# Retention and two feed-forward layers: loads in rows of 2 KB, a new order of the beginning, zeros in wide products

## The chip, the cores and the metric

One core of one Trainium2 chip. The metric is the device time of one execution in microseconds (us), median of several runs. TensorE is called PE, VectorE DVE, ScalarE ACT, GpSimd POOL, SyncE SP; SP issues nearly all DMAs.

## The reference

Retention (attention without softmax, with a decaying causal mask) for 4 batches, 8 heads, 576 positions, head size 64, then two feed-forward layers on the 2304 tokens with 512 features and 2048 hidden values. All inputs are float32.

```python
scores = q @ k.T / sqrt(64)
ret = scores * where(rel >= 0, gamma[h] ** rel, 0)
x = (ret @ v) as tokens x 512
h = x @ w_in;  g = maximum(0.01 * h, h);   x = g @ w_out      # layer 1
h = x @ w_in2; g = h * cos(h);             out = g @ w_out2   # layer 2
```

## The kernel before, in words

Tokens go through retention in 18 chunks of 128 (ch0 to ch17), the first layer in 5 blocks of up to 512 tokens and 16 slices of the hidden width (f = 0 to 15), the second layer by a scheme with fewer products, whose operands are sums of quarters. Each float32 operand of a feed-forward product is split into a high and a low part of a rounded type, and one product is three (low times high, high times low, high times high). The weights arrive as 64-bit words that ACT and DVE turn into these parts.

The order of the instructions of each engine up to the end of the first block is written out by hand as a table of step names, FIRST; each name issues a few instructions, and the engines run them in that order, held by semaphores alone. What follows is set by a planner, which the change leaves as it is. The steps, for chunk or slice n:

- ch: load of a chunk (lines 238 to 241): q, k in two layouts and v, 1 MB; chunk 0 in two halves. sq, sv: scaling of q and v (lines 247 and 254 or 259).
- s: scores on PE (line 295), 16 products of 64x64. m: times the mask, on DVE (line 316). v: mask times values, PE (line 333). g: growth of the state, PE (line 357). st: the state's sum, DVE (lines 379 and 381). r: what the queries read of the state, PE (line 396) in two parts, with an empty GpSimd instruction behind each part that orders them (line 282). tk: result from PSUM to SBUF, ACT (line 435).
- raw, abs, lo, cs, or, add, hi, low: load of a weight slice (lines 463 and 468; slices 0 and 15 in halves a and b), and its change into parts: abs, lo and hi on ACT (lines 479, 483, 512), cs, or, add and low on DVE (lines 487 and 489, 496, 503, 515).
- xh, xl: high and low part of the layer's input (lines 527 on ACT, 531 on DVE). H: first product of slice n (line 543). lk, gh, gl: the nonlinearity and its parts (lines 568 and 573 on ACT, 578 on DVE). O: second product (line 557). V: a whole retention chunk between products.
- ~n: n products of zeros that only keep PE busy (line 453).

A matmul on float32 leaves two matmul and two weight-load records in the trace, one on the rounded type one of each.

Of the kernel before, what the change touches and what calls it, by code (L numbers as in the profile page):

```python
# [11 lines left out]
I64 = mybir.dt.int64  # L12
# [23 lines left out]
C = P // 2  # L36
# [14 lines left out]


FIRST = """
ch0 sq0 sv0 s0 m0 raw0a abs0a cs0a ~3 v0 or0a ch1 sq1 g0 ch2 ~5 s1 st0.0 st0.1 r0.0 r0 lo0a add0a m1 sv1 v1
sq2 s2 g1 hi0a low0a m2 sv2 v2 g2 ch3 sq3 s3 st1.0 st1.1 r1.0 r1 m3 sv3 v3 g3 raw0b tk0 abs0b cs0b st2.0 st2.1
lo0b or0b add0b r2.0 r2 st3.0 st3.1 tk1 raw1 abs1 cs1 lo1 or1 add1 ~3 r3.0 tk2 r3 tk3 xh0 xl0 ~14 H0.0 xh1 xl1
H0.1 xh2 xl2 H0.2 hi0b low0b xh3 xl3 hi1 low1 raw2 raw3 raw4 ch4 abs2 cs2 H0.3 H1.0 H1.1 H1.2 H1.3 lk0 gh0
abs3 gl0 or2 lo2 add2 lk1 gh1 gl1 sq4 O0 O1 hi2 low2 H2.0 H2.1 H2.2 H2.3 cs3 or3 lo3 add3 abs4 cs4 sv4 V3 raw5
raw6 raw8 hi3 low3 lk2 H3.0 H3.1 H3.2 H3.3 gh2 gl2 O2 or4 lo4 add4 abs5 cs5 hi4 low4 raw7 lk3 gh3 gl3 or5 lo5
add5 abs6 cs6 H4.0 H4.1 H4.2 H4.3 O3 raw9 ch5 lo7 hi5 low5 or6 lk4 gh4 gl4 lo6 add6 H5.0 H5.1 H5.2 H5.3 O4  # L60
st4.0 sq5 hi6 low6 abs7 cs7 lk5 gh5 gl5 or7 add7 m4 H6.0 H6.1 lo8 abs8 st4.1 H6.2 H6.3 lk6 gh6 O5 gl6 O6 hi7
low7 cs8 or8 add8 raw10 abs9 cs9 raw11 raw15a raw12 H7.0 H7.1 H7.2 H7.3 sv5 V4 hi8 lo9 low8 or9 add9 lk7 gh7
gl7 abs10 cs10 hi9 low9 H8.0 H8.1 H8.2 H8.3 lk8 gh8 or10 gl8 st5.0 O7 lo11 abs11 cs11 lo10 add10 ch6 H9.0 H9.1
H9.2 H9.3 lk9 m5 gh9 O8 gl9 O9 hi10 low10 st5.1 raw13 or11 sv6 add11 sq6 tk4 abs12 cs12 H10.0 H10.1 H10.2
H10.3 hi11 V5 ch7 lk10 lo12 low11 m6 st6.0 gh10 gl10 lo13 lo15a H11.0 H11.1 H11.2 H11.3 lk11 gh11 abs13 or12
add12 hi12 gl11 O10 O11 st6.1 cs13 low12 raw15b raw14 or13 add13 H12.0 H12.1 H12.2 H12.3 tk5 sq7 sv7 V6 hi13
low13 abs14 cs14 lk12 lo14 gh12 gl12 or14 add14 H13.0 H13.1 H13.2 H13.3 abs15a lk13 lo15b gh13 gl13 O12 O13
hi14 low14 abs15b st7.0 cs15a cs15b st7.1 m7 or15a tk6 ch8 H14.0 H14.1 H14.2 H14.3 add15a hi15a low15a sq8 sv8
V7 st8.0 or15b lk14 gh14 gl14 st8.1 add15b H15.0 H15.1 H15.2 H15.3 lk15 gh15 gl15 hi15b low15b tk7 O14 O15 m8
ch9 sq9 sv9  # L70
"""


# [99 lines left out]
def retention_ffn_ffn(  # L173
# [7 lines left out]
    nc = tc.nc  # L181
# [31 lines left out]
    tabs_sb = const.tile([P, sum(sizes)], F32, name="tabs_sb")  # L213
# [6 lines left out]
    still = const.tile([P, P], F32, name="still")  # L220
    psum = psp.tile([P, 8, 512], F32, name="psum")
# [3 lines left out]
    n_first = len(chunks[0])  # L225
    n_busy = n_first + len(chunks[1])
# [22 lines left out]
    def scale_v(i):  # L249
        c = i % CYCLE * H  # L250
        if i in (1, 2) or n_first <= i < n_busy:
            for h in range(H):
                v = ch_t[i][:, 3, h * D : (h + 1) * D]
                nc.scalar.activation(v, v, AF.Copy, scale=vtab_sb[:, c + h : c + h + 1])
            return
        v3 = ch_t[i][:, 3].rearrange("p (h d) -> p h d", h=H)
        t3 = vtab_sb[:, c : c + H].unsqueeze(2).to_broadcast([P, H, D])
        eng = nc.gpsimd if 0 < i < n_busy + 2 else nc.vector
        eng.tensor_tensor(out=v3, in0=v3, in1=t3, op=ALU.mult)

    xr, p_t, summed = {}, {}, {}
# [15 lines left out]
    def in_turn(ins, behind):  # L277
        tc.add_manual_dep(ins.ins, behind.ins.name, IN_TURN, reason="same banks")
# [7 lines left out]
    last_of = {}  # L286
# [350 lines left out]
    for j in range(NB - 1):  # L639
        s1 = NF * j + FIRST_CHUNK  # L640
# [4 lines left out]
    def rest():  # L645
# [3 lines left out]
        bank = [psum[:, x, :W] for x in range(8)]  # L649
# [387 lines left out]
        def convert(f, c, tb, due, old):  # L1037

            rb, o = raw_ring.next(), c % 2 * 2 * P
            t_of = lambda: tb.ap[:, o : o + 2 * P]  # L1040
            sides = lambda: rb.ap.bitcast(U32).rearrange("p (x t) -> p x t", t=2)
            lo, hi = lambda: sides()[:, :, 0], lambda: sides()[:, :, 1]

            def load():
                nc.sync.dma_start(rb.ap.bitcast(I64), w[1, f, :, c * 2 * P : (c + 1) * 2 * P])

            def both(op):
                u = t_of().bitcast(U32)
# [24 lines left out]
            return t
# [461 lines left out]
```

## Time and profile before

| | |
|---|---|
| median of 3 runs | 841.66 us (838.97 to 842.35) |
| the profiled execution's own time | 840.51 us |
| its span, first to last instruction | 838.4 us |
| mean granted PE clock | 0.992 |
| PE busy | 812.5 us |
| DVE, ACT busy | 647.3 us, 543.7 us |
| POOL busy | 6.2 us |

The span is what the views below measure; 2.1 us of the execution lie around it. A busy share is an average over stages with different limits: the change touches the first tenth of the span most.

### The profile page before, as it was taken

Reading aid. Unit: us, or ns where it says so; the run is one execution under the profiler, and the core shown is the slowest. Engines: PE = TensorE matmul, PEld = TensorE weight load, DVE = VectorE, ACT = ScalarE, POOL = GpSimd, SP = SyncE. Lnnn points to the kernel's source line nnn. Section 1 sums busy time; section 2 is a strip of 40 time slices with the busy share of each in tenths; the row PEclk is TensorE's granted clock in tenths of the full one; section 3 lists DMA queues with packets and bytes.
Section 4 is the critical chain, followed back from the end, with each engine's and each line's share of the span. In section 5 each row is a group of like instructions: output and inputs, shape, how many; then the busy total and the mean of one; then the engine's idle time right before and its main releaser. Section 6 shows DMA issues by size and latency. Waiting matters only on the chain.

```text
span 838.4 us, 16145 instructions
## 1 busy us (share of the span) xinstructions
PE 812.5 (97%) x6168; PEld 746.0 (89%) x6168; DVE 647.3 (77%) x1147; ACT 543.7 (65%) x1041; POOL 6.2 (1%) x9
## 2 busy tenths in 40 slices
PE   6999999999999999999999998999999999999996
PEld 4877878887888888999999998999999999999996
DVE  4899987887886867786741278799896988877994
ACT  4687866655655456565542498877778876688761
POOL 0000011000000000000000000000000000000000
PEclk9799999999999999999999999999999999999999
DMA  8755325877778767876679499888866677465633
GB/s 319 297 206 208 140 107 189 260 244 215 264 238 254 249 214 258 262 233 217 209 246 416 154 333 328 299 318 312 291 228 254 242 314 289 156 256 197 257 138 114
DMA packets 88636, 203.78 MB, mean 243 GB/s; under 512 B 9072, under 2 KB 54896, under 8 KB 79472
## 3 DMA queue, kind: packets, MB, share of 16 engines
q1 hardware_dynamic: 88416, 202.41, 68.7%
q8 instruction: 48, 0.79, 0.4%
q10 hardware_dynamic: 144, 0.35, 0.1%
q14 instruction: 28, 0.23, 0.1%
HBM read 147.42 MB, written 55.31 MB: 242 GB/s over the span
## 4 chain that ended last, share of the span: by engine, by line
PE 66%; DMA 12%; DVE 11%; ACT 5%; issue 3%; SPq 2%; POOL 0%; DVEq 0%; ACTq 0%; POOLq 0%
PE psum L1362 19%; PE psum L1190 18%; PE psum L543 13%; PE psum L557 13%; DMA more<-in_w 2%; DMA ch<-in_qkv 2%; DMA mraw<-in_w 2%; SPq L933 1%; DMA mt<-y 1%; DMA y<-graw 1%; PE psum L396 1%; DMA ws<-ws 1%; DMA xq<-mt 1%; PE psum L333 1%; PE psum L453 1%
## 5 line engine op out<-in xcount | busy, mean ns | idle before, releaser
L543 PE MATMUL psum<-x_sb,w 128*128 128x512 f32 (+1 forms) x960 | 212.3, 370 | 2.1 <-ACT graw L837 1.4
L557 PE MATMUL psum<-g,w 128*128 128x512 f32 (+1 forms) x960 | 211.9, 370 | 1.2 <-DVE graw L800 0.6
L543 PEld LDWEIGHTS psum<-x_sb,w 128*128 128x128 f32 x960 | 174.5, 188 | 28.2 <-ACT graw L837 2.8
L557 PEld LDWEIGHTS psum<-g,w 128*128 128x128 f32 x960 | 174.1, 188 | 26.5 <-DVE graw L800 1.4
L1190 PE MATMUL psum<-x,ws 128*128 128x384 f32 x576 | 112.2, 335 | 3.6 <-DMA ws<-ws 2.1
L1190 PEld LDWEIGHTS psum<-x,ws 128*128 128x128 f32 x576 | 100.7, 188 | 5.0 <-DMA ws<-ws 2.5
L1362 PE MATMUL psum<-g,wp 128*128 128x384 f32 x432 | 84.4, 339 | 4.0 <-ACT g L1265 2.1
L1190 PE MATMUL psum<-x,wa 128*128 128x384 f32 x432 | 85.5, 335 | 0.5 <-ACT r L1245 0.5
L844 DVE TENSOR_TENSOR g<-graw,g 128x512 fp32r<-128x512 f32 (+1 forms) x64 | 39.8, 622 | 56.5 <-ACT g L841 55.8
L1362 PE MATMUL psum<-g,wq 128*128 128x384 f32 x432 | 82.3, 334 | 0.1
L1362 PEld LDWEIGHTS psum<-g,wp 128*128 128x128 f32 x432 | 75.9, 189 | 6.2 <-ACT g L1265 2.4
L1190 PEld LDWEIGHTS psum<-x,wa 128*128 128x128 f32 x432 | 75.7, 188 | 1.1 <-ACT r L1245 0.8
L1362 PEld LDWEIGHTS psum<-g,wq 128*128 128x128 f32 x432 | 75.5, 188 | 0.4 <-DVE acc L1399 0.4
L837 ACT ACTIVATE graw<-psum 128x512 f32<-128x512 f32 (+1 forms) x64 | 34.7, 542 | 48.9 <-PE psum L543 45.0
L841 ACT CAST g<-graw 128x512 fp32r<-128x512 f32 (+1 forms) x64 | 36.2, 566 | 43.3 <-PE psum L557 43.1
L1399 DVE TENSOR_TENSOR acc<-psum,acc 128x384 f32<-128x384 f32 x90 | 49.6, 554 | 17.2 <-PE psum L1362 16.9
L1248 DVE SCALAR_TENSOR_TENSOR h<-r,h 128x768 f32<-128x768 f32 x48 | 45.7, 952 | 15.2 <-ACT r L1245 15.1
L1261 DVE TENSOR_TENSOR g<-tq,g 128x768 fp32r<-128x768 f32 x48 | 45.6, 953 | 6.8 <-ACT g L1265 6.2
L1239 DVE SCALAR_TENSOR_TENSOR r<-r,h 128x768 f32<-128x768 int32 x48 | 45.5, 951 | 1.9 <-ACT r L1234 1.6
L1244 ACT ACTIVATE r<-r 128x768 f32<-128x768 f32 x48 | 40.6, 847 | 8.7 <-DVE r L1239 8.6
L1234 ACT CAST r<-h 128x768 int32<-128x768 f32 x48 | 40.1, 835 | 8.2 <-DVE h L1220 7.9
L1265 ACT CAST g<-tq 128x768 fp32r<-128x768 f32 x48 | 40.1, 838 | 5.7 <-DVE tq L1282 4.2
(115 smaller groups left out, 1061.0 us busy)
## 6 DMA issues: line engine op xcount, KB each, us to landing
ws<-ws SPq DMA_DIRECT2D x20, 1024.0 KB, 5.2
wp<-wp SPq DMA_DIRECT2D x20, 1024.0 KB, 6.7
ch<-in_qkv SPq DMA_DIRECT2D x17, 1024.0 KB, 6.4
x<-xq SPq DMA_DIRECT2D x21, 768.0 KB, 9.7
wa<-wa SPq DMA_DIRECT2D x20, 768.0 KB, 6.4
wq<-wq SPq DMA_DIRECT2D x20, 768.0 KB, 6.6
raw<-in_w SPq DMA_DIRECT2D x14, 1024.0 KB, 8.8
mraw<-in_w SPq DMA_DIRECT2D x32, 256.0 KB, 4.2
```

Of the source, the lines that this page charges most:

```text
L543: nc.tensor.matmul(hp, wt[:, i, cols], x_t[lj, k][:, j, :n], start=(k == 0 and a == 0), stop=(k == KK - 1 and a == 2),)
L557: nc.tensor.matmul(psum[:, BANK_O + m, :n], wt[:, i, cols], gt[:, j, :n], start=(f == 0 and a == 0), stop=(f == NF - 1 and a == 2),)
L844: nc.vector.tensor_tensor(out=g.ap[:, 1, :n], in0=y.ap[:, :n], in1=g.ap[:, 0, :n].bitcast(F32), op=ALU.subtract)
L1190: nc.tensor.matmul(bank[BANKS[m]].rearrange("p (q t) -> p q t", t=Q), a[:, hl, i, j * P : (j + 1) * P], x[:, :, v, j, :], start=m in (1, 5 ...
L1234: "ACT", 885, lambda: nc.scalar.copy(rb.ap.bitcast(I32), pair()),
L1239: nc.vector.scalar_tensor_tensor(out=rb.ap, in0=rb.ap.bitcast(I32), scalar=-1.0, in1=pair(), op0=ALU.mult, op1=ALU.add)
L1244: t = add("ACT", 885, lambda: nc.scalar.activation(rb.ap, rb.ap, AF.Sin, scale=PI), [t], due)
L1248: nc.vector.scalar_tensor_tensor(out=pair(), in0=rb.ap, scalar=0.5, in1=pair(), op0=ALU.subtract, op1=ALU.mult)
L1261: nc.vector.tensor_tensor(out=gb.ap[:, :, 1], in0=src(), in1=gb.ap[:, :, 0].bitcast(F32), op=ALU.subtract)
L1265: h_ = add("ACT", 885 if n == 2 else 515, lambda: nc.scalar.copy(gb.ap[:, :, 0], src()), [*needs, opened["all"]], due, 0, gb.old)
L1362: nc.tensor.matmul(to, wt[:, hl, i, t * P : (t + 1) * P], gt[:, fi, v, :], start=m in (1, 5) and h == 0 and x == 0, stop=h == 1 and x == 2 ...
L1399: x = add("DVE", 560, lambda: nc.vector.tensor_tensor(out=kept(), in0=to, in1=kept(), op=ALU.add), [got], due - SOON / 2)
```

## The change

Five things. The host lays chunks and weights out in blocks, so that a load of 1 MB takes four rows of 2 KB for each partition from four places, where it took one row of 8 KB (halves: two rows of 2 KB, not one of 4 KB). A second-layer load of 256 KB, which took rows of 2 KB out of rows of 8 KB, now takes one contiguous block. The table FIRST has another order. The load of chunk 4 gets an order behind the last growth product issued so far. The scaling of chunk 3's v goes from GpSimd to DVE. And zeros are multiplied up to 512 columns at a time, with the tables as the moving operand (the stationary one is zero).

```diff
-            nc.sync.dma_start(ch[:, :2], qkv[i, :, :2])
-            nc.sync.dma_start(ch[:, 2:], qkv[i, :, 2:])
+            nc.sync.dma_start(ch[:, :2], qkv[i, :2].rearrange("x p d -> p x d"))
+            nc.sync.dma_start(ch[:, 2:], qkv[i, 2:].rearrange("x p d -> p x d"))
         else:
-            nc.sync.dma_start(ch, qkv[i])
+            got = nc.sync.dma_start(ch, qkv[i].rearrange("x p d -> p x d"))
+            if i == n_first:
+                in_turn(got, last_of["grown"])
...
-        eng = nc.gpsimd if 0 < i < n_busy + 2 else nc.vector
+        eng = nc.gpsimd if n_busy <= i < n_busy + 2 else nc.vector
...
-        for _ in range(n):
-            nc.tensor.matmul(psum[:, bank, :P], still, still, start=True, stop=True)
+        while n > 0:
+            c = min(n, 4) * P
+            nc.tensor.matmul(psum[:, bank, :c], still, tabs_sb[:, C : C + c], start=True, stop=True)
+            n -= 4
...
-        return nc.sync.dma_start(raw, w[0, f])
+        return nc.sync.dma_start(raw.rearrange("p (c t) -> p c t", c=4), w[0, f].rearrange("c p t -> p c t"))
...
-        return nc.sync.dma_start(raw, w[l, f, :, s * DM : (s + 1) * DM])
+        return nc.sync.dma_start(
+            raw.rearrange("p (c t) -> p c t", c=2), w[l, f, 2 * s : 2 * s + 2].rearrange("c p t -> p c t")
+        )
...
-                nc.sync.dma_start(rb.ap.bitcast(I64), w[1, f, :, c * 2 * P : (c + 1) * 2 * P])
+                nc.sync.dma_start(rb.ap.bitcast(I64), w[1, f, c])
...
-ch0 sq0 sv0 s0 m0 raw0a abs0a cs0a ~3 v0 or0a ch1 sq1 g0 ch2 ~5 s1 st0.0 st0.1 r0.0 r0 lo0a add0a m1 sv1 v1
+ch0 sq0 s0 sv0 m0 raw0a abs0a cs0a or0a ~3 v0 g0 st0.0 st0.1 ~4 r0.0 ch1 sq1 s1 r0 lo0a add0a ch2 m1 sq2 sv1
...
```

The order of PE from the scores of chunk 2 on, before (L295 scores, L333 values, L357 growth, L396 reads, L453 zeros):

```order
L295 MATMUL psum<-ch 64x64 x16
L357 MATMUL psum<-ch 64x64 x16
L333 MATMUL psum<-p_sb,ch 64x64 x16
L357 MATMUL psum<-ch 64x64 x16
L295 MATMUL psum<-ch 64x64 x16
L396 MATMUL psum<-ch,st 64x64 x16
L333 MATMUL psum<-p_sb,ch 64x64 x16
L357 MATMUL psum<-ch 64x64 x16
L396 MATMUL psum<-ch,st 64x64 x16
L453 MATMUL psum<-still 128x128 x3
L396 MATMUL psum<-ch,st 64x64 x16
L453 MATMUL psum<-still 128x128 x14
```

And in the changed kernel, from the same scores on (there L297, L335, L359, L398 and L456):

```order
L297 MATMUL psum<-ch 64x64 x16
L398 MATMUL psum<-ch,st 64x64 x8
L335 MATMUL psum<-p_sb,ch 64x64 x16
L398 MATMUL psum<-ch,st 64x64 x8
L359 MATMUL psum<-ch 64x64 x16
L297 MATMUL psum<-ch 64x64 x16
L398 MATMUL psum<-ch,st 64x64 x16
L335 MATMUL psum<-p_sb,ch 64x64 x16
L359 MATMUL psum<-ch 64x64 x16
L456 MATMUL psum<-tabs_sb,still 128x512
L456 MATMUL psum<-tabs_sb,still 128x128
L398 MATMUL psum<-ch,st 64x64 x16
```

The scores of chunk 3 are the second row of scores in each list. The reads of chunk 1 and all growth of chunk 2 now stand ahead of them; zeros that stood in three and fourteen products of 128 columns stand in four of 512 and two of 128, the last four of the six behind these rows.

The order of DVE around the mask multiply of chunk 3 (L316), before; L247 is q's scaling, L381 the state's sums, t_426 and t_464 the weights of slice 0's second half and slice 1 on their way:

```order
L316 TENSOR_TENSOR p_sb<-psum,tabs_sb 128x512
L247 TENSOR_TENSOR ch<-ch,tabs_sb 128x512
L381 TENSOR_TENSOR st<-psum,st 128x256 x2
L316 TENSOR_TENSOR p_sb<-psum,tabs_sb 128x512
L487 TENSOR_SCALAR t_426<-t_426 128x512
L489 TENSOR_SCALAR t_426<-t_426 128x512
L381 TENSOR_TENSOR st<-psum,st 128x256 x2
L496 SCALAR_TENSOR_TENSOR t_426<-raw,t_426 128x512
L503 ISA t_426<-raw,t_426 128x1024
L381 TENSOR_TENSOR st<-psum,st 128x256 x2
```

And in the changed kernel (mask L318, scaling L249 and L261, sums L383; the weights are t_394 and t_477):

```order
L318 TENSOR_TENSOR p_sb<-psum,tabs_sb 128x512
L249 TENSOR_TENSOR ch<-ch,tabs_sb 128x512
L261 TENSOR_TENSOR ch<-ch,tabs_sb 128x512
L383 TENSOR_TENSOR st<-psum,st 128x256 x2
L318 TENSOR_TENSOR p_sb<-psum,tabs_sb 128x512
L494 TENSOR_SCALAR t_394<-t_394 128x512
L496 TENSOR_SCALAR t_394<-t_394 128x512
L503 SCALAR_TENSOR_TENSOR t_394<-raw,t_394 128x512
L510 ISA t_394<-raw,t_394 128x1024
L383 TENSOR_TENSOR st<-psum,st 128x256 x2
```

Two pairs of state sums and the scaling of chunk 3's v now stand ahead of the mask multiply of chunk 3; one pair stands behind it, where two stood.

DVE somewhat later, before: L531 is xl, L515 the low part of a weight slice, L578 the low part of the nonlinearity's result, L247 the scaling of chunk 4:

```order
L531 TENSOR_TENSOR x_sb<-xr,x_sb 128x512 x3
L515 TENSOR_TENSOR w_296<-t_426,w_296 128x512
L531 TENSOR_TENSOR x_sb<-xr,x_sb 128x512
L515 TENSOR_TENSOR w_536<-t_464,w_536 128x1024
L487 TENSOR_SCALAR t_547<-t_547 128x1024
L489 TENSOR_SCALAR t_547<-t_547 128x1024
L578 TENSOR_TENSOR g<-graw,g 128x512
L496 SCALAR_TENSOR_TENSOR t_547<-raw,t_547 128x1024
L503 ISA t_547<-raw,t_547 128x2048
L578 TENSOR_TENSOR g<-graw,g 128x512
L247 TENSOR_TENSOR ch<-ch,tabs_sb 128x512
L515 TENSOR_TENSOR w_606<-t_547,w_606 128x1024
```

And in the changed kernel (L538, L522, L585, L249):

```order
L538 TENSOR_TENSOR x_sb<-xr,x_sb 128x512 x2
L249 TENSOR_TENSOR ch<-ch,tabs_sb 128x512
L538 TENSOR_TENSOR x_sb<-xr,x_sb 128x512 x2
L522 TENSOR_TENSOR w_509<-t_477,w_509 128x1024
L494 TENSOR_SCALAR t_516<-t_516 128x1024
L496 TENSOR_SCALAR t_516<-t_516 128x1024
L585 TENSOR_TENSOR g<-graw,g 128x512
L503 SCALAR_TENSOR_TENSOR t_516<-raw,t_516 128x1024
L510 ISA t_516<-raw,t_516 128x2048
L585 TENSOR_TENSOR g<-graw,g 128x512
```

The scaling of chunk 4 has moved from behind two results of the nonlinearity to between the second and the third low part of x.

## Rows read from the trace of the kernel before

**Rows 1.** The page: PE's busy time and instructions, and the instruction queue (packets, MB, share).

```profile
PE 812.5 (97%) x6168; PEld 746.0 (89%) x6168; DVE 647.3 (77%) x1147; ACT 543.7 (65%) x1041; POOL 6.2 (1%) x9
...
q8 instruction: 48, 0.79, 0.4%
```

**Rows 2.** Busy us by engine (PE, weight loads, DVE, ACT, POOL), granted clock, DMA share, GB/s.

```profile
0.00:9.88 9.88, 6.97 (x93) 3.82 (x96) 2.71 (x6) 2.29 (x4) 0.20 (x4) 1.00 0.79 282
0.00:15.30 15.30, 11.12 (x218) 7.33 (x221) 7.79 (x15) 6.31 (x18) 0.20 (x4) 1.00 0.87 330
0.00:18.51 18.51, 13.78 (x348) 9.61 (x348) 9.91 (x19) 8.38 (x26) 0.20 (x4) 1.00 0.89 335
...
22.20:32.40 10.20, 9.28 (x162) 8.26 (x163) 9.27 (x15) 6.82 (x17) 1.04 (x1) 0.50 0.59 212
50.67:86.25 35.58, 35.58 (x255) 28.43 (x256) 34.35 (x40) 28.61 (x40) 0.00 (x0) 1.00 0.42 153
86.25:838.40 752.15, 735.61 (x5253) 684.96 (x5251) 576.90 (x1055) 483.47 (x934) 4.99 (x4) 1.00 0.70 242
```

**Rows 3.** PE in order of time: start, duration, line, operation, records, idle time before.

```profile
17.94 0.57 PE L295 MATMUL psum<-ch 64*64 64x64 f32 x22
...
21.52 0.38 PE L295 MATMUL psum<-ch 64*64 64x64 f32 x9 [3.02 <-issue]
...
29.79 4.64 PE L453 MATMUL psum<-still 128*128 128x128 f32 x28
...
50.67 2.83 PE L543 MATMUL psum<-x_sb,w 128*128 128x512 f32 x11 [0.39 <-DVE w L515]
```

**Rows 4.** DMA view of 12.9:14.0, 15.3:19.2, 19.2:20.4 and 23.1:24.3, in this order.

```profile
q8 instruction: 1, 0.02, 5.4%
...
q1 hardware_dynamic: 264, 1.44, 101.6%
...
q8 instruction: 1, 0.02, 5.0%
...
q8 instruction: 1, 0.02, 4.8%
```

**Rows 5.** DMA view of 30:34 (8 KB rows), 131.1:132 (2 KB rows), 140:141.2 (2 KB rows, with stores).

```profile
DMA packets 230, 1.70 MB, mean 426 GB/s; under 512 B 22, under 2 KB 22, under 8 KB 22
...
DMA packets 93, 0.33 MB, mean 366 GB/s; under 512 B 16, under 2 KB 16, under 8 KB 65
...
q1 hardware_dynamic: 93, 0.33, 89.7%
...
DMA packets 239, 0.44 MB, mean 364 GB/s; under 512 B 26, under 2 KB 26, under 8 KB 239
```

**Rows 6.** DVE in order of time, columns as in PE's.

```profile
9.79 0.43 DVE L487 TENSOR_SCALAR t<-t 128x512 f32<-128x512 f32 x1 [0.71 <-ACT t L479]
...
17.19 0.69 DVE L247 TENSOR_TENSOR ch<-ch,tabs_sb 128x512 f32<-128x512 f32 x1 [0.70 <-DMA ch<-in_qkv]
...
22.00 0.69 DVE L316 TENSOR_TENSOR p_sb<-psum,tabs_sb 128x512 f32<-128x512 f32 x1 [3.26 <-PE psum L295]
...
22.61 1.13 DVE L487 TENSOR_SCALAR t<-t 128x512 f32<-128x512 f32 x1
...
26.84 0.95 DVE L381 TENSOR_TENSOR st<-psum,st 128x256 f32<-128x256 f32 x2 [0.35 <-PE psum L396]
...
38.54 0.69 DVE L578 TENSOR_TENSOR g<-graw,g 128x512 fp32r<-128x512 f32 x1 [1.32 <-ACT g L573]
...
40.62 1.23 DVE L503 CUSTOM_DVE_ANT_0 t<-raw,t 128x2048 uint16<-128x2048 uint16 x1 [0.25 <-ACT raw L483]
...
49.40 1.22 DVE L515 TENSOR_TENSOR w<-t,w 128x1024 fp32r<-128x1024 f32 x1
```

**Rows 7.** GpSimd in order of time.

```profile
22.41 1.04 POOL L259 TENSOR_TENSOR ch<-ch,tabs_sb 128x512 f32<-128x512 f32 x1 [21.97 <-PE psum L396]
```

**Rows 8.** DMA view of 25.5:25.9: a load issued on an idle queue, median us to landing.

```profile
raw<-in_w SPq DMA_DIRECT2D x1, 1024.0 KB, 5.5
```

More of the change, by code (lines that the diff above doesn't have):

```diff
@@ L53 @@
 FIRST = """
-ch0 sq0 sv0 s0 m0 raw0a abs0a cs0a ~3 v0 or0a ch1 sq1 g0 ch2 ~5 s1 st0.0 st0.1 r0.0 r0 lo0a add0a m1 sv1 v1
[L55 to L68, printed above, removed]
@@ L69 @@
-V7 st8.0 or15b lk14 gh14 gl14 st8.1 add15b H15.0 H15.1 H15.2 H15.3 lk15 gh15 gl15 hi15b low15b tk7 O14 O15 m8
-ch9 sq9 sv9
+ch0 sq0 s0 sv0 m0 raw0a abs0a cs0a or0a ~3 v0 g0 st0.0 st0.1 ~4 r0.0 ch1 sq1 s1 r0 lo0a add0a ch2 m1 sq2 sv1
+hi0a low0a v1 g1 s2 st1.0 st1.1 r1.0 sv2 m2 v2 r1 ch3 sq3 sv3 raw0b raw1 tk0 g2 st2.0 st2.1 s3 m3 abs0b tk1
+cs0b or0b lo0b add0b r2.0 r2 v3 g3 st3.0 st3.1 ~5 r3.0 r3 abs1 cs1 or1 lo1 hi0b low0b add1 tk2 tk3 xh0 xl0 xh1
+xl1 ch4 sq4 xh2 xl2 xh3 xl3 hi1 low1 raw2 raw3 abs2 cs2 ~13 H0.0 H0.1 H0.2 H0.3 H1.0 H1.1 H1.2 H1.3 lk0 gh0
@@ new lines @@
+gl0 lo2 abs3 or2 add2 lk1 gh1 O0 gl1 O1 cs3 hi2 low2 H2.0 H2.1 H2.2 H2.3 sv4 V3 raw4 lo3 or3 add3 abs4 cs4 hi3
+low3 raw5 raw7 raw6 raw8 ch5 raw9 raw15a or4 lk2 gh2 gl2 lo4 add4 abs5 cs5 H3.0 H3.1 H3.2 H3.3 O2 hi4 lk3 low4
+H4.0 H4.1 H4.2 H4.3 gh3 gl3 O3 lo5 or5 add5 abs6 cs6 hi5 lk4 gh4 low5 H5.0 H5.1 H5.2 H5.3 gl4 O4 lo7 lo6 abs7
+or6 add6 cs7 hi6 low6 lk5 gh5 gl5 or7 add7 H6.0 H6.1 H6.2 H6.3 O5 abs8 cs8 hi7 lk6 low7 H7.0 H7.1 H7.2 gh6 gl6
+st4.0 or8 lo8 add8 st4.1 raw10 lo10 sq5 raw11 H7.3 lk7 gh7 gl7 m4 O6 O7 hi8 low8 H8.0 H8.1 abs9 abs10 lo9 sv5
@@ new lines @@
+cs9 or9 add9 raw12 cs10 hi9 low9 H8.2 H8.3 V4 ch6 or10 lk8 gh8 st5.0 gl8 st5.1 add10 abs11 cs11 H9.0 H9.1 H9.2
+H9.3 lk9 gh9 gl9 O8 O9 or11 tk4 hi10 low10 H10.0 H10.1 H10.2 H10.3 raw15b raw13 lo11 add11 raw14 sv6 sq6 m5 V5
+ch7 abs12 hi11 lk10 gh10 cs12 low11 gl10 or12 lo12 add12 lo13 abs13 H11.0 H11.1 H11.2 H11.3 lk11 gh11 hi12 sv7
+lo14 cs13 gl11 st6.0 m6 st6.1 sq7 O10 O11 tk5 low12 H12.0 or13 add13 hi13 H12.1 H12.2 H12.3 lk12 gh12 abs14
+low13 abs15a gl12 V6 st7.0 st7.1 cs14 or14 H13.0 H13.1 H13.2 H13.3 add14 lk13 gh13 gl13 O12 O13 cs15a hi14
@@ L71 @@
+low14 or15a abs15b tk6 lo15b cs15b ch8 H14.0 H14.1 H14.2 H14.3 sq8 sv8 lo15a m7 add15a hi15a low15a V7 st8.0
+lk14 gh14 gl14 st8.1 tk7 H15.0 H15.1 H15.2 H15.3 O14 lk15 or15b add15b gh15 gl15 hi15b low15b O15 m8 ch9 sq9
+sv9
 """
@@ L1500 @@
     parts += [tokens(a).reshape(NCH, P, DM) for a in (k, v)]
-    arrays = {"in_qkv": np.ascontiguousarray(np.stack(parts, axis=2))}
+    arrays = {"in_qkv": np.ascontiguousarray(np.stack(parts, axis=1))}
     layers = []
@@ L1508 @@
         w_out = inputs[f"{name}_w_out"].reshape(NF, P, DM)
-        layers.append(np.concatenate([w_in, w_out], axis=2))
+        layers.append(np.concatenate([w_in, w_out], axis=2).reshape(NF, P, 4, 2 * P).transpose(0, 2, 1, 3))
     arrays["in_w"] = np.ascontiguousarray(np.stack(layers)).view(np.int64)
```

## The prediction

> **What bounds the kernel now.** I read the page first, then PE's busy time by stretches, then PE's timeline of the first 50 us, and last the DVE timeline of the same stretch. PE is busy 97% of the span [rows 1]. From 50.67 to 86.25 us it has no idle time at all, and from 86.25 to the end it is busy 735.61 of 752.15 us [rows 2]. So whatever moves PE's first products of the first layer earlier moves the end by nearly the same amount, and what the change does to transfers behind that point costs nothing as long as PE finds its data there.
>
> The beginning is another matter. The first product with weight tile 3 (step H3, line 543) runs at full pace only from 50.67, released by DVE's subtraction of line 515 [rows 3, 6]. In front of that lies the largest stall. At 18.51 PE stops in the middle of the scores of chunk 3 (32 records, of which 22 have run), and it goes on at 21.52, 3.02 us later, with the releaser "issue": no semaphore that the profile shows ended it [rows 3].
>
> Count instructions: PE plus weight-load records are 189 at 9.88, 439 at 15.30 and 696 at 18.51 [rows 2], so they are some 250 apart. On the instruction queue q8 one packet starts behind each of these: one between 12.9 and 14.0, none between 15.3 and 19.2, one between 19.2 and 20.4, one between 23.1 and 24.3 [rows 4]. Over the span q8 has 48 packets for 2 x 6168 records [rows 1], 257 for each. I read this so: at each boundary of about 256 instructions PE asks for the block after the next one, and at 18.51 the block asked for at 15.3 has not come. By its share of the window a packet takes 5.4% x 1.1 us x 16 = 0.95 us [rows 4], so the second one ends near 20.3, and PE runs 1.2 to 1.3 us later. From asking to running on: 9.88 to about 13.95 + 1.3 = 15.25, that is 5.4 us; 15.3 to 21.52, 6.2 us, both behind 8 KB rows; on an idle queue 21.52 to 24.1 + 1.3, 3.9 us.
>
> **The change, part by part.**
>
> *Rows of 2 KB.* In a stretch of 8 KB rows alone the queue moves 426 GB/s [rows 5]. With 2 KB rows I have two bounds: 366 GB/s at 89.7% busy, 408 at full, and 364 in a stretch in which stores run too [rows 5]. So a load is 4 to 17% longer. Chunk 3, released at 17.19 [rows 6] after some 15 us of queue, comes 0.6 to 2.5 us later. That is hidden by the missing block as long as the scores of chunk 3 can't run before about 21; if that cover went, up to 2 us of it would show. I take 1 us, the end nearer to the load-only row: the scores could then start at 18.9. For the second layer's 256 KB loads the rows stay at 2 KB and only lie together: nothing, either way, since PE's waits there are not for them.
>
> *What the rows do to the fetch.* Bounds: 6.2 us as now, 3.9 us as on an idle queue. I take 5.4 us, the better of the two loaded fetches.
>
> *Zeros in wide products.* 25 narrow products of 4 records (two matmuls, two weight loads) become 8: 68 instructions fewer. In the new order 688 instructions stand ahead of the scores of chunk 3 (before: 652), so the block boundary near 700 falls at their start, not in their middle; the one at about 952 falls on the reads of chunk 3. The stall isn't ordered away. The columns are nearly the same (13 x 128 ahead of H0, 14 x 128 before), so as time they cost what they did.
>
> *The order.* The boundary near 448 is again crossed in the scores of chunk 2, at about 15.6 (15.3, with chunk 2 some 0.3 us later). Plus 5.4: the scores of chunk 3 run from 21.0. They need 0.7 us, so the mask multiply (m3, line 316) starts on DVE at 21.75, against 22.00 [rows 6].
>
> From there DVE sets the pace up to H3: in the old trace from 22.00 to 49.40 + 1.22 = 50.62, 28.62 us [rows 6]. In this chain:
> - one pair of state sums (as the one at 26.84, 0.95 us, about 0.9 of it in the chain) now stands ahead of m3, since the reads of chunk 1 precede the scores of chunk 3: -0.9;
> - the clamp at 22.61 takes 1.13 us where the same form takes 0.43 [rows 6], beside GpSimd's multiply at 22.41 [rows 7]; v's scaling goes to DVE, ahead of the scores, where DVE waits anyway: -0.7;
> - the wait of 0.35 at 26.84 for the reads of chunk 2, which are now done long before: -0.35;
> - the wait of 1.32 at 38.54 is for ACT's rounding of H0's result. H0 started only after the fourteen zero products, at 34.4 (29.79 + 4.64), because they ran at half clock: 22.20 to 32.40 is 0.50 granted [rows 2, 3]. With the clock up the zeros end about 8.5 us after m3 (worked out with the first rival) and H0 is done before DVE comes to it: -1.32; the wait of 0.25 at 40.62 goes with the earlier weights: -0.25.
> - Chunk 4's q scaling is in the chain before and after, only earlier: 0.
>
> Sum: -3.5, so 25.1 us, and H3 runs from 21.75 + 25.1 = 46.9 instead of 50.67: 3.8 us. Behind it PE has no idle time to lose or win up to 86 us, and the order of PE's products is the same from about 80 us on. The profiled execution took 840.51 (838.4 and 2.1 around it), 1.15 below the median of 841.66; it becomes 836.7, and the median **837.9**.
>
> **The rivals.**
>
> *The clock falls as before.* PE still idles, by my sum, from 18.9 to 21.0, and a shorter wait for the reads' block follows near 24. [...] Of the fourteen's 4.64 us, 2.6 lay before 32.40 and 2.0 behind [rows 2, 3], so one costs 0.24 at full clock and 0.48 at half. With the clock up PE needs 8.5 us from m3 to the zeros' end: reads, values and growth of chunks 2 and 3 some 4.2, eighteen zero products' worth of columns 4.3. DVE's turn at H0's result was 15.2 us behind m3 (38.54 less 1.32 and 22.00 [rows 6]); less 0.9, 0.7 and 0.35, plus 0.6 for chunk 4's scaling, it is 13.9, and H0 with ACT's two passes takes 4.1, so H0 has 1.3 us to spare. At half clock throughout it is 3.0 us late; with the clock back at 32.40, 1.9. I take 2.5: gain 3.8 - 2.5 = 1.3, median 840.4. For it: this is what followed 3.02 us of idle time. Against: the idle time is a third shorter, and reads and values follow it at once.
>
> *The fetch is no quicker, or the stop has another cause.* With 6.2 us m3 is at 22.55 and H3 at 47.65, gain 3.0: 838.7; together with the fallen clock 841.2. If something else than a missing block stops PE in these scores and does so for 3.0 us again, it is from 18.9 to 21.9, and the time is the same within 0.1. For that: nothing in the trace names the cause. Against: the packet whose end lies 1.2 us ahead of the restart [rows 3, 4]. [...] The stop right there speaks against it, so I give that half of it 0.03.
>
> *The fetch is as quick as on an idle queue.* 3.9 us: block there at 19.5, scores then, m3 at 20.25, H3 at 45.35: gain 5.3, 836.3. [...] Against: of the two fetches behind 8 KB rows one was 0.8 us quicker than the other, so row size isn't all of the wait.
>
> *Slower.* The load of chunk 4 now waits for the growth products of chunk 3 and then stands ahead of the weights; its q scaling stands on DVE between x's second and third low part, in front of everything that H0 to H3 need. Issued at about 24.6, with the 5.5 us that a load on an idle queue takes [rows 8] it is there at 30.1; DVE comes to it about 31.8 (13.9 us behind m3 less 3.8 of work between). From 1.7 us later on, DVE and all behind it wait one for one: the gain of 3.8 is gone when the chunk lands 5.5 us late. For it: loads here have taken far longer behind others. Against: it is at the head of an empty queue. At 10 us late: 837.9 + 8.3 = 846.2.
>
> **How the numbers follow.** My forecast 0.45, clock falls 0.25, fetch no quicker (with or without the clock) 0.12, quick fetch 0.12, slower 0.06. The forecast's own range is 836.5 to 839.5, by a fetch of 5 to 6 us. For 8 in 10 I take 835.3 (the quick fetch, and the sum's waits a little larger) to 841.2 (fallen clock and a fetch no quicker). About 0.5%, 4.2 us, is what a measurement of this kernel can tell from no change; that is below 837.5. The quick fetch and the better two fifths of the forecast are there: 0.33. Slower by that takes the last rival and little else: 0.06. The rest is 0.61.
>
> **What would show it.** Right: PE's "issue" wait at the scores of chunk 3 is near 2 us instead of 3; a q8 packet starts between 18 and 19; no multiply on GpSimd near 22; m3 at 21 to 22; the wait of line 578's successor for ACT is gone; the first 12 products of H3 run from about 47; the clock's row has no 0.50 after 20 us. Wrong: a granted clock of 0.50 between 22 and 32 again; DVE waiting for chunk 4 (line 249) near 31; a wait for chunk 3 on DVE past 20 us, which would mean that the rows, not the fetch, set the pace.

## The result, and the profile after

The changed kernel took **833.56 us** (median of 6 runs, 832.62 to 833.90), the kernel before 841.42 beside it (838.97 to 843.06): ratio 0.991, 95% interval 0.989 to 0.993. It is faster by 7.9 us. The forecast of 837.9, a gain of 3.8 us, had the sign and half of the size, and its range (835.3 to 841.2) missed the time. The profiled execution of after took 833.8, its span is 831.7.

Busy time of after by stretches, columns as in [rows 2]:

```profile
18.50:22.20 3.70, 1.30 (x85) 1.17 (x78) 1.33 (x3) 2.23 (x6) 0.00 (x0) 1.00 0.37 130
22.87:26.28 3.41, 3.41 (x82) 2.77 (x83) 3.10 (x7) 2.26 (x4) 0.00 (x0) 0.50 0.00 0
22.20:32.40 10.20, 9.56 (x159) 6.43 (x151) 9.47 (x15) 8.01 (x16) 0.00 (x0) 0.83 0.58 202
50.67:86.25 35.58, 35.58 (x260) 29.33 (x259) 34.51 (x42) 27.68 (x38) 0.00 (x0) 1.00 0.46 155
86.25:831.70 745.45, 733.18 (x5241) 684.76 (x5239) 574.61 (x1051) 482.85 (x933) 5.61 (x4) 1.00 0.70 245
```

The granted clock is at 0.50 for 3.4 us, where the kernel before had 10.2 us of it [rows 2]. And behind 86.25 PE is idle 12.27 us; before it was 752.15 - 735.61 = 16.54 [rows 2]. The forecast had nothing there, and these 4.3 us are the larger part of the 6.7 by which the two spans differ. PE of after in order of time:

```profile
19.07 0.28 PE L297 MATMUL psum<-ch 64*64 64x64 f32 x2
...
21.74 0.63 PE L297 MATMUL psum<-ch 64*64 64x64 f32 x27 [2.40 <-issue]
...
27.99 3.06 PE L456 MATMUL psum<-tabs_sb,still 128*128 128x512 f32 x8
31.38 1.66 PE L550 MATMUL psum<-x_sb,w 128*128 128x512 f32 x6 [0.33 <-DVE x_sb L538]
...
47.90 3.37 PE L550 MATMUL psum<-x_sb,w 128*128 128x512 f32 x12
```

The stop stands where the instruction count put it, after 2 records of the scores of chunk 3 (line 297) instead of 22 [rows 3], and ends 0.22 us later than it did before. The last row is step H3: its first product runs at 47.90, the rest of it from 48.46, behind DVE's subtraction; that is 2.2 us ahead of [rows 3]. DVE of after, and behind it ACT:

```profile
22.49 0.69 DVE L318 TENSOR_TENSOR p_sb<-psum,tabs_sb 128x512 f32<-128x512 f32 x1 [2.23 <-PE psum L297]
23.10 0.42 DVE L494 TENSOR_SCALAR t<-t 128x512 f32<-128x512 f32 x1
...
35.84 0.69 DVE L494 TENSOR_SCALAR t<-t 128x1024 f32<-128x1024 f32 x1 [0.83 <-ACT t L486]
...
47.18 1.22 DVE L522 TENSOR_TENSOR w<-t,w 128x1024 fp32r<-128x1024 f32 x1
```

```profile
34.68 1.13 ACT L486 ACTIVATE t<-raw 128x1024 f32<-128x1024 f32 x1 [2.40 <-DMA raw<-in_w]
```

The mask multiply (first row) came 0.49 us later than in [rows 6] and the last subtraction ended 2.2 us earlier. The clamp took 0.42 instead of 1.13, and the wait of 1.32 for H0's result is gone. New is 0.83 at 35.84: weight tile 2 stands behind chunk 4 in the queue.

### The profile page after: what moved, and what is told of

The parts are those of the page before. It is cut to its first block, busy times and chain, and to the rows that moved or that the text cites. A ratio compares the mean times of both kernels' runs of the same rounds, so it can differ in the third digit from the quotient of the medians.

```text
span 831.7 us, 16073 instructions
## 1 busy us (share of the span) xinstructions
PE 810.5 (97%) x6134; PEld 742.4 (89%) x6134; DVE 647.2 (78%) x1148; ACT 543.8 (65%) x1041; POOL 5.8 (1%) x8
## 4 chain that ended last, share of the span: by engine, by line
PE 81%; DVE 8%; DMA 4%; issue 3%; ACT 3%; SPq 0%; DVEq 0%; POOLq 0%; ACTq 0%
PE psum L564 20%; PE psum L550 20%; PE psum L1369 19%; PE psum L1197 19%; DMA ch<-in_qkv 1%; DMA raw<-in_w 1%; PE psum L335 1%; DVE w L522 1%; PE psum L359 1%; DMA ws<-ws 1%; PE psum L398 1%; DVE t L510 1%; DVE t L503 1%; DVE g L1268 1%; PE psum L297 1%
```

## The experiments

Times are medians of 5 to 12 executions; "before" is the kernel before in the same comparison. The executions of one kernel spread over 1.3 to 9 us, and an interval reaches 1.5 to 3.5 us to either side. The ratio is taken over all executions, not from the two medians: by it layer2_only gains 0.1 to 3.0 us, wide_only 1.8 to 4.8, and tail_only cannot be told from no change.

| kernel | us | before | ratio, 95% interval |
|---|---|---|---|
| layer2_only | 836.82 | 839.49 | 0.998 (0.996 to 1.000) |
| rows_only | 837.53 | 839.49 | 0.998 (0.996 to 0.999) |
| order_only (with wide zeros) | 832.86 | 839.49 | 0.994 (0.992 to 0.996) |
| after_l2_old | 832.97 | 839.49 | 0.994 (0.992 to 0.996) |
| head_only | 836.05 | 840.04 | 0.996 (0.994 to 0.999) |
| tail_only | 838.17 | 840.04 | 0.999 (0.996 to 1.001) |
| fetch_first | 831.49 | 840.04 | 0.989 (0.985 to 0.993) |
| fetch_split | 835.52 | 840.88 | 0.993 (0.990 to 0.995) |
| after_again | 831.11 | 840.88 | 0.990 (0.987 to 0.993) |
| after_8kb | 832.41 | 840.88 | 0.991 (0.988 to 0.994) |
| after_narrow | 835.41 | 840.88 | 0.994 (0.992 to 0.997) |
| wide_only | 837.21 | 840.01 | 0.996 (0.994 to 0.998) |
| order_narrow | 837.75 | 840.01 | 0.998 (0.996 to 0.999) |
| fetch_mid | 830.57 | 840.01 | 0.988 (0.986 to 0.991) |

**Which part gives the gain.** My first theory (A) was that the second layer's contiguous loads give what the forecast lacked behind 86 us; rivals were the order (B) and the rows of the chunks and first-layer weights (C).

layer2_only and after_l2_old differ in effect in one load, with the host's layout for it, from the kernels before and after:

```
-  nc.sync.dma_start(rb.ap.bitcast(I64), w[1, f, :, c * 2 * P : (c + 1) * 2 * P])   # strided
+  nc.sync.dma_start(rb.ap.bitcast(I64), w[1, f, c])                                # contiguous
```

> The kernel before, in which only the second layer's 256 KB loads read contiguous blocks (old order, old rows, narrow zeros). Theory A (the 3.9 us gained behind 86 us come from these loads landing earlier, 3.6 us after issue instead of 4.2): about 2.5 us faster than before. Rival B (they come from the order, whose table reaches to about 128 us, and from everything starting earlier): no change. Rival C (they come from the 2 KB rows of chunks and first-layer weights): no change.

> The changed kernel, in which only the second layer's loads are strided again (2 KB rows out of 8 KB). Theory A: about 2.5 us slower than the changed kernel, 836. Rivals B and C: as the changed kernel, 833.6.

Measured: 2.7 us by the medians on the old order, and taken out of the changed kernel it costs nothing that can be told (832.97 against 833.56 and 831.11). A falls as the main cause.

rows_only has all new layouts with the old table, narrow zeros and GpSimd's scaling; order_only the new table, wide zeros, DVE's scaling and chunk 4's order with all old layouts:

```
 rows_only:   FIRST, fill, eng, in_turn of before;  load_chunk, load_raw, load_half, rb of after
 order_only:  FIRST, fill, eng, in_turn of after;   load_chunk, load_raw, load_half, rb of before
```

> All new layouts (2 KB rows, contiguous second-layer blocks) with the old order, narrow zeros and GpSimd's scaling. Theory A: 2 to 3 us faster than before. Rival B: the same or up to 1 us slower, since 2 KB rows load more slowly. Rival C: 3 us faster or more.

> The new order, wide zeros, chunk 3's scaling on DVE and chunk 4's load behind the growth products, but all loads in the old rows and the old layout. Theory A: 3 to 4.5 us faster than before (2.9 of the beginning and the 1.3 at 123 us). Rival B: 7 us faster, as the changed kernel. Rival C: 2 to 4 us faster.

Measured: 2.0 and 6.6 us. Order and zeros together make nearly all of the gain; the layouts add little to them. rows_only has the second layer's blocks too and gains no more than layer2_only, so C falls. B is left, as far as these four go; it holds the zeros, DVE's scaling and chunk 4's order as well, of which only the zeros were tried alone.

**Beginning or rest of the table.** head_only and tail_only cut the table at step H2.3, old layouts in both:

```
 head_only:  FIRST = new[: H2.3] + "raw4" + old[H2.3 :] without cs3;  fill, eng, in_turn of after
 tail_only:  FIRST = old[: H2.3] + "cs3" + new[H2.3 :] without raw4;  fill, eng, in_turn of before
```

> The kernel before with the new order up to step H2.3 and what goes with it (wide zeros, v scaling of chunks 1 to 3 on DVE, chunk 4's load behind the growth products), old rows, and the old order behind H2.3. If the beginning makes the gain, 833 to 835 (the order with both parts had 832.9), and PE's 1.57 us of idle time at 124 us is gone or small although the old order stands there. If the order behind the beginning makes the larger part, the idle time near 124 is there again and the time is 836 to 837.5.

> The kernel before with the old order up to H2.3 and the new one behind it (to about 128 us), old rows, old zeros. If the beginning makes the gain, 838.5 to 839.5, as the kernel before. If the order behind it gives the 1.3 us at 124 us and leaves ACT and DVE earlier for what follows, 835.5 to 837.5, with no idle time at 124 and none at 208.

Measured: 4.0 and 1.9 us, the sum about that of order_only; the 1.9 are not clear of the spread. The wait near 124 us belongs to the old rest of the table. PE of before, of head_only, then of tail_only:

```profile
125.25 0.69 PE L333 MATMUL psum<-p_sb,ch 64*64 64x64 f32 x32 [1.57 <-ACT xr L435]
```

```profile
123.88 0.69 PE L340 MATMUL psum<-p_sb,ch 64*64 64x64 f32 x32 [1.28 <-ACT xr L442]
```

```profile
121.04 2.80 PE L549 MATMUL psum<-x_sb,w 128*128 128x512 f32 x11 [0.48 <-DVE w L521]
```

With the old rest it is there in every profile (1.23 to 1.57), with the new one in none, whatever stands in front. In its place most profiles with the new rest show smaller waits for DVE between 116 and 136 us, so that PE's idle time from 86 to 200 us is 0.05 to 1.28 there, against 1.27 to 1.88 with the old rest. For head_only I expected the gain of the beginning to shrink the wait at 124 too; it did not. For tail_only I expected no idle time near 208; it has 0.42 there, behind ACT.

**The kernel before, once more.** No edit.

> The kernel before, profiled a second time. Asked: do PE's idle times at 208.66 us (0.94, released by ACT) and at 336 to 338 us (0.49 and 0.62) and the clock's 0.50 from 22.2 to 32.4 belong to the kernel or to that one execution? If to the kernel, all three come again within some tenths. If to the execution, PE has under 0.3 us of idle time between 200 and 400 us, as the four variants have, and H3 starts up to 1.7 us earlier, at 49.0, as in the variant that differs from this kernel in the second layer's layout alone.

It took 839.74. PE's waits from 200 to 400 us, with sum, times and longest:

```profile
PE psum L557 <- DVE graw L800: 0.3, 1, 0.3
PE psum L543 <- ACT graw L837: 0.2, 1, 0.2
```

In the first profile the same places cost 1.1 and 1.4 us: PE was idle 2.70 of these 200 us there, 0.68 here, and 0.16 in layer2_only, rows_only, order_only and head_only. So most of that was the execution. But not all executions are alike in this: over the 17 profiles it is above 1 us in four of the eight whose second-layer loads are strided (2.70 in the first profile of before, 2.09 in tail_only, 1.55 in wide_only, 1.11 in order_narrow) and at most 0.56 in the nine whose loads are contiguous. So the layout seems to make such waits rarer. PE at the first of them in the first profile, and what ACT waited for just ahead:

```profile
209.60 3.01 PE L543 MATMUL psum<-x_sb,w 128*128 128x512 f32 x12 [0.94 <-ACT graw L837]
```

```profile
ACT more L1064 <- DMA more<-in_w: 3.4, 1, 3.4
```

That is a load of the second layer. The long stretch of 0.50 came again (10.2 us from 22.3, after 3.4 us ahead of the stop), and H3 was at 51.01. A profile whose beginning is the same but whose low clock near 23 us was short shows its price: layer2_only has 3.4 us of it and H3 at 49.02, 1.65 ahead of [rows 3] (0.11 of that because its stop ended earlier). So the low stretch differs in length between executions with the same beginning.

PE of layer2_only at H3:

```profile
49.02 2.82 PE L550 MATMUL psum<-x_sb,w 128*128 128x512 f32 x11 [0.40 <-DVE w L522]
```

**The zeros.** after_narrow and order_narrow are the changed kernel and order_only with narrow zeros, wide_only the kernel before with wide ones:

```
-        while n > 0:
-            c = min(n, 4) * P
-            nc.tensor.matmul(psum[:, bank, :c], still, tabs_sb[:, C : C + c], start=True, stop=True)
-            n -= 4
+        for _ in range(n):
+            nc.tensor.matmul(psum[:, bank, :P], still, still, start=True, stop=True)
```

> The changed kernel with the zeros in narrow products as before: one wide product (4 records with its weight loads) becomes four narrow ones, so 20 instructions more ahead of the scores of chunk 3. If the stop is a block that is late, it moves ahead with the count, from the scores of chunk 3 to the growth products of chunk 2 (line 359 or the states before them), and starts about 0.3 us earlier; from there on the order is the same. Time: 833.6 to 834.3, that is the wide products give nothing by themselves. If the stop belongs to the scores of chunk 3, it stays there.

PE of after_narrow:

```profile
18.66 0.56 PE L359 MATMUL psum<-ch 64*64 64x64 f32 x24
21.69 0.36 PE L359 MATMUL psum<-ch 64*64 64x64 f32 x8 [2.48 <-issue]
21.82 1.11 PE L297 MATMUL psum<-ch 64*64 64x64 f32 x32
```

20 instructions more in front, and the stop is exactly 20 earlier: 2 records of line 297 and 8 of line 359, each with its weight load. So it belongs to the count and not to a step. DVE's pair of state sums, ahead of the stop in the changed kernel, now waits behind it (3.07 at 22.07), the mask multiply is at 22.98 instead of 22.49, and H3's first product at 48.66 instead of 47.90, both profiles with 3.4 us of low clock. That is 0.8 us. The median was 4.3 us above after_again and 1.9 above the first median of the changed kernel, where I had expected no difference.

> The kernel before with the zeros in wide products and nothing else. 20 instructions fewer stand ahead of the scores of chunk 3, so the block boundary, in the middle of them before (22 of 32 records run), falls 10 records later: at their very end or at the state products behind them. If the wide products count only through that boundary, DVE's mask multiply is early but its state sums still wait, and the time is 838 to 840, within half a microsecond of the kernel before. If they are worth something by themselves (the changed kernel with narrow ones took 835.4 against 831.1 beside it), 836 to 837.5.

> The new order with the old rows (832.9) and the zeros in narrow products. The stop moves from the scores of chunk 3 to the growth products of chunk 2, as with the new rows. If the wide products are worth 3 to 4 us on the new order, 836 to 837; if the 4 us seen with the new rows was the spread between executions, 832.5 to 834.

Measured: the wide zeros alone give 2.8 us on the old order; without them the new order gives 2.3 instead of 6.6. PE at the stop and at H3, and DVE of wide_only:

```profile
21.89 0.46 PE L402 MATMUL psum<-ch,st 64*64 64x64 f32 x16 [2.96 <-issue]
...
49.41 2.83 PE L552 MATMUL psum<-x_sb,w 128*128 128x512 f32 x11 [0.39 <-DVE w L524]
```

```profile
19.00 0.69 DVE L322 TENSOR_TENSOR p_sb<-psum,tabs_sb 128x512 f32<-128x512 f32 x1
19.61 0.42 DVE L496 TENSOR_SCALAR t<-t 128x512 f32<-128x512 f32 x1
20.06 0.43 DVE L498 TENSOR_SCALAR t<-t 128x512 uint32<-128x512 uint32 x1
23.02 0.95 DVE L387 TENSOR_TENSOR st<-psum,st 128x256 f32<-128x256 f32 x2 [2.54 <-PE psum L402]
...
26.99 0.95 DVE L387 TENSOR_TENSOR st<-psum,st 128x256 f32<-128x256 f32 x2 [1.58 <-PE psum L402]
```

The boundary has moved 10 records on, to the very end of the scores (32 of 32). The stop is as long as ever (2.96 us, 3.02 in [rows 3]), but behind them: the mask multiply and two clamps run during it (the multiply at 19.00, not 22.00). The lead does not last. The state sums wait 2.54 and 1.58 for PE's reads, as I had expected. H0 starts at 32.57 instead of 34.19 and H3 at 49.41 instead of 50.67, but this profile has only 3.4 us of low clock near 23 us, and layer2_only, with narrow zeros and as much of it, has H0 at 32.18 and H3 at 49.02. So the 2.8 us of the medians are not seen in the beginning, and where on the old order they come from stays open.

**What sets the length of the stop.** In the changed kernel SP issues two loads of 0.5 and 1 MB, half of weight tile 0 and tile 1, at 13.09 and 13.51, and PE asks for its block at about 15.7 (an estimate by the instruction count, 441 records at 15.74). Three kernels hold these loads:

```
             if n == 1 or n == 0 and half:
-                in_turn(got, last_of["scores", 1])
+                in_turn(got, last_of["scores", 2])                # fetch_first: both
+                in_turn(got, last_of["scores", 3 if n else 1])    # fetch_split: tile 1 (raw1 after s3 in FIRST)
+                in_turn(got, last_of["scores", 2 if n else 1])    # fetch_mid: tile 1
```

> The changed kernel, with the loads of weight tile 0's second half and of tile 1 held until the scores of chunk 2 (they waited for those of chunk 1), so that they stand behind the request for PE's next block, not in front of it. If the queue's load sets how long a block takes, the block asked for at about 15.7 us comes in 3.9 us as on an idle queue: the scores of chunk 3 run on from 19.6 instead of 21.74, the issue wait is under 0.7 us (2.40), m3 is at 20.4 on DVE, H3's products at 46.5 to 47.0 instead of 47.9 to 48.5, and the time is 1 to 1.9 us less: 831.7 to 832.6. If a block takes 6 us whatever stands in the queue, the issue wait stays at 2.4 and the time at 833.6; if the held loads are late instead, ACT waits for tile 0's second half near 23 and the gain is less.

PE of fetch_first, and its ACT:

```profile
19.25 0.68 PE L297 MATMUL psum<-ch 64*64 64x64 f32 x32
...
27.55 0.80 PE L456 MATMUL psum<-tabs_sb,still 128*128 128x128 f32 x2 [3.99 <-issue]
```

```profile
25.69 1.12 ACT L486 ACTIVATE t<-raw 128x1024 f32<-128x1024 f32 x1 [3.22 <-DMA raw<-in_w]
```

The stop at the scores is gone, all 32 records run at 19.25: the block's packet started 0.7 us after the request, at 16.65 (at 19.22 in after). The stop came back one block later, behind the held loads, and tile 1 was late for ACT (22.21 in after). H3 was at 49.37 in this profile, later than in after; the median of 831.49 is that of after_again, and the execution profiled was the slowest of the five (835.03).

> The changed kernel with one load moved: that of weight tile 1 waits for the scores of chunk 3 (not chunk 1); tile 0's second half stays where it was. Then only half a megabyte stands in front of the block asked for at 15.7 us, and nothing in front of the one asked for at about 19.3. If loads in front of the request set how long a block takes: no issue wait over 0.6 us before H0 (the changed kernel 2.40 at the scores of chunk 3, the kernel with both loads held 3.99 at the zeros), m3 at 20.4 to 21.0 on DVE, H3's products from 46 to 47.3 instead of 47.9, time 831 to 832.5. If a block takes about 6 us anyway and the two loads together only shifted which block was late: a wait of 2 us or more at the scores or at the zeros, time 833 to 834. The cost to look for: ACT waiting for tile 1 past 25 us.

PE of fetch_split, and its ACT:

```profile
32.91 8.58 PE L550 MATMUL psum<-x_sb,w 128*128 128x512 f32 x24 [3.69 <-DVE x_sb L538]
```

```profile
26.65 1.15 ACT L486 ACTIVATE t<-raw 128x1024 f32<-128x1024 f32 x1 [5.34 <-DMA raw<-in_w]
```

No stop at all, as expected, and yet the median is 4.4 us above after_again: tile 1 came at 26.65 (22.21 in after), DVE waited for it, and H0 waited for DVE. The size is uncertain, since the executions of the two overlap (831.64 to 836.48 and 830.35 to 835.31) and the slowest was profiled; the wait is plain. The fetch alone is not the bound of the beginning; the first weights are the other half.

> The changed kernel with one wait moved: the load of weight tile 1 waits for the scores of chunk 2 (not chunk 1, and not chunk 3 as in the run before). Both late things of the earlier runs should be gone: half a megabyte in front of the block asked for at 15.7 us (its packet then started at 17.5, and no issue wait followed), and tile 1 issued near 16.7 should land near 22.5 to 23.5 (5.5 us on an idle queue, 26.65 in the run before). If the beginning is bound by these two alone, m3 is at 20.4 to 21.2 on DVE, tile 1's clamps at 24.3 to 25 (26.3 in the changed kernel), H3's products at 46 to 47, and the time 829.5 to 831. If one of the two loads still makes a block late, or tile 1 lands past 25, the time is that of the changed kernel, 831 to 833.6.

DVE and PE of fetch_mid, and its stretches:

```profile
20.45 0.69 DVE L318 TENSOR_TENSOR p_sb<-psum,tabs_sb 128x512 f32<-128x512 f32 x1
...
24.27 0.68 DVE L494 TENSOR_SCALAR t<-t 128x1024 f32<-128x1024 f32 x1
```

```profile
19.70 0.69 PE L297 MATMUL psum<-ch 64*64 64x64 f32 x30 [0.27 <-issue]
...
23.71 0.49 PE L456 MATMUL psum<-tabs_sb,still 128*128 128x128 f32 x2 [0.24 <-issue]
...
45.10 3.40 PE L550 MATMUL psum<-x_sb,w 128*128 128x512 f32 x12
```

```profile
22.20:32.40 10.20, 8.58 (x71) 4.85 (x63) 9.89 (x15) 8.25 (x17) 0.00 (x0) 1.00 0.86 301
```

Both late things are gone, everything came as expected, H3 even at 45.10, and the clock stayed at 1.00. At 830.57 it is the fastest version here, 3 us below the changed kernel (0.5 below after_again, within the spread).

**The rows of 2 KB.** after_8kb is the changed kernel with 8 KB rows for chunks and first-layer weights, in effect:

```
-            got = nc.sync.dma_start(ch, qkv[i].rearrange("x p d -> p x d"))
-        return nc.sync.dma_start(raw.rearrange("p (c t) -> p c t", c=4), w[0, f].rearrange("c p t -> p c t"))
+            got = nc.sync.dma_start(ch, qkv[i])
+        return nc.sync.dma_start(raw, w[0, f])
```

> The changed kernel with the chunks and the first layer's weights laid out as before (rows of 8 KB, 4 KB for half loads); the second layer's loads stay contiguous. If the 2 KB rows are worth nothing by themselves, the time is that of the changed kernel or up to 1 us less, as a load of 1 MB then takes 2.49 us and not 2.70: 832 to 833.6. If they make the fetch quicker, the issue wait is 2.9 us or more (2.40 in the changed kernel, 2.86 in the kernel with the new order and all the old rows) and the time 834 to 835.

> The changed kernel again, beside the others of this call and profiled a second time: 833.6 within 1 us; PE's issue wait at the start of the scores of chunk 3 again (2.2 to 3.4), no idle time over 0.6 near 124, 208 or 336 us.

PE of after_8kb:

```profile
23.30 1.02 PE L303 MATMUL psum<-ch 64*64 64x64 f32 x27 [3.56 <-issue]
```

With the new order the scores run on at 22.90 to 23.30 with the old rows (order_only, head_only, after_8kb), at 21.47 to 22.02 with the new ones (after, after_again, after_l2_old): the rows bring the block 1.4 us earlier (averages 23.16 and 21.74). On the old order they do not: there it is 22.41 with the new rows (rows_only) and 21.41 to 21.91 with the old ones. And even on the new order the median of after_8kb is 1.3 us above after_again and 1.2 below the first median of after: as time of the whole, it can't be told from nothing. after_again was 2.4 us below that first median; its stop was 1.09 instead of the 2.2 to 3.4 that I expected, and H3 ran at 47.27, although its clock was at 0.50 for 10.2 us, from 14.60 on. So differences of that size between comparisons of one kernel must be allowed for.

## Why the prediction was half right

*The stop and its place.* Right. Its place follows the count, to the instruction, in after_narrow. That is what speaks against another cause: the stop in before came at record 696 [rows 2], and the packets are 257 records apart [rows 1]. Its length is not fixed: stops of 1.09 to 3.99 us here, and waits of at most 0.27 when the large load ahead of the request is held back to the right place (fetch_mid).

*Length of the fetch, 5.4 us.* Mis-sized: 21.74 - 15.74 = 6.0. The start of the packet went with the bytes in front: it came at 19.22 with 1.5 MB of loads issued there (after), at 17.14 to 17.54 with 0.5 MB (fetch_mid, fetch_split), at 16.65 with none of the two loads (fetch_first). In after q8 has no row in 15.7:19.1, where q1 is busy all the time (104.5%, 1.31 MB). DMA view of after in 19.1:19.4, at the end of the loads, and of fetch_mid in 17:17.3, where q1 is nearly idle:

```profile
q1 hardware_dynamic: 59, 0.12, 108.8%
q8 instruction: 1, 0.02, 23.0%
```

```profile
q8 instruction: 1, 0.02, 23.0%
q1 hardware_dynamic: 9, 0.01, 11.5%
```

Rows a quarter as long helped by 1.4 us on the new order and did not make the wait a quarter as long, so the rival of the quick fetch did not come true through the rows; through the order of the loads it did (19.25 for the scores in fetch_first, 19.5 in the rival).

*Sum of DVE's chain, 25.1 us.* 22.49 to 48.40 is 25.9. Each term was seen (the clamp at 0.42, the pair of sums ahead of the multiply, the wait for H0 gone). Missing was the 0.83 that tile 2 loses behind chunk 4: the place of the slower rival, at a tenth of its price. With the 0.74 of the later multiply this gives the 1.5 us by which H3 was late against the forecast (46.9, seen 48.4).

*The clock.* It fell, for a third as long. The rival had 2.5 us for the whole stretch; layer2_only shows 1.65 for 10.2 against 3.4 us of it. So most of the 2.2 us that H3 won may be that: beside layer2_only, with the old beginning and as much low clock, the changed kernel's H3 (48.46) is 0.6 us ahead. Where the stretch lies counts too: in after_again it was 10.2 us long, began ahead of the stop, and H3 came 0.6 us earlier than in after.

*"25 narrow products become 8 ... as time they cost what they did."* **The step that failed, first.** The term was put at nothing, and the medians give the wide zeros 2.8 us on the old order (wide_only) and 1.9 to 4.9 on the new (after_narrow, order_narrow). I counted the instructions and asked only whether the stop would go away, not which work of DVE would then stand ahead of it. On the new order that is shown, and is 0.8 us at H3 (after_narrow against after; 1.4 against after_again; 1.5 in order_narrow against order_only, with 3.4 us more of low clock). On the old order the boundary moves too, and layer2_only shows nothing won by it at H3. So the boundary explains a part, and the rest of the price is open. In after_narrow some more is lost from 119 to 139 us (1.0 against after, 0.2 against after_again), where PE waits 0.63 and 0.32 for DVE. What is seen of the rest is behind 500 us, below.

*"Behind it PE has no idle time to lose or win up to 86 us".* **The second.** True of these 36 us, but the sum ended there, and the same group of rows had 16.54 us of idle time behind it, of which the changed kernel has 12.27. 1.57 of it, at 124 us behind ACT, went with the rest of the new table (tail_only), which I had read as an order without effect since PE's own does not change behind 80 us. *"PE's waits there are not for them"*, of the second layer's loads, was wrong too: at 208.66 PE waited for ACT and ACT 3.4 us for such a load. layer2_only and rows_only are 2 to 2.7 us faster by their medians; on the new order the loads' layout adds nothing that can be told.

*What stays open.* Against the first profile of before, order_only has a lead of 2.5 us at 157 us, 5.5 at 362 and 7.6 at 641; before_again leads it by 2.2 between the first two as well. So part of what the two profiles show behind 200 us is the spread of executions and not the change. And near 500 to 571 us the granted clock is at 0.50 for 3.4 us in some profiles: in 5 of the 7 with narrow zeros, in 2 of the 10 with wide ones, and where it came in order_narrow the lead over before fell from 3.3 us at 553 to 1.9 at 579. That would explain why the medians give the wide zeros more than the beginning does; what brings it about there was not tried. A difference of the clock is there in all executions, not only in those profiled: its mean over the span, averaged over a kernel's executions, is 0.990 to 0.991 with narrow zeros (0.994 in after_narrow alone) and 0.992 to 0.996 with wide ones. From 0.990 to 0.994 is 3.4 us of 838, an estimate of the most that it can be worth, if PE is the bound wherever the clock is low.

## What to carry to other kernels

Count instructions as well as time: here a block of instructions that was late stopped PE for 1.09 to 3.99 us at a place that followed from the count, and 20 instructions fewer ahead of it changed which work of the other engines still got done before the stop. Then ask what that work's successors wait for: on the old order here the early work led straight into the next wait (the mask multiply 3.0 us earlier, then 2.54 and 1.58 for PE's reads in wide_only). Look at what stands in the queues when the block is asked for, and hold a load back until the request has gone in front, but only as long as its own reader allows (in fetch_mid tile 1 came in time and the median was 830.57; in fetch_split ACT had it at 26.65 and the median was 835.52). When a sum stops at the first stretch without idle time, say what idle time lies behind it and who ends it. And before a difference between two profiles is put down to the change, look whether the clock was low for as long in both (10.2 us against 3.4 here, 1.65 us at H3).

## What was not expected of the hardware

SP's loads in 2 KB rows hold the issuing queue much longer. SP of after:

```profile
25.32 0.37 SPq L241 DMA_DIRECT2D ch<-in_qkv  x1
25.73 13.16 SPq L468 DMA_DIRECT2D raw<-in_w  x7
```

Seven issues take 13.16 us; the last four of them take 2.4 to 2.6 us each, a megabyte apiece, nearly as long as the transfer itself (an estimate: 2.70 us at the 388 GB/s that 30 to 42 us show, 2.49 at 421 with 8 KB rows in order_only). With the old rows one took 0.33 to 1.57 (before, from 25.56 on), and order_only's seven 4.37 in all.

A fetch of 16 KB (0.79 MB in 48 packets, [rows 1]) waited behind the loads that were issued before it, although it has a queue of its own (q8; the loads are on q1): 0.7 us from request (placed by the count) to packet with neither load in front, 3.5 with 1.5 MB there. In after q1 moved 1.31 MB in 15.7:19.1, and no packet of q8 came between. Why the fetch waits for loads on another queue, these runs do not show.
